# Attention scores in slots of three units instead of two, in a fused threshold-attention and SwiGLU kernel

## The chip, the cores and the metric

One core of a Trainium2 chip (trn2) runs the whole program. The metric is device time in microseconds (us). TensorE is called PE in the profile, and its weight loads PEld; VectorE is DVE, ScalarE is ACT, GpSimd is POOL, and SP issues the DMAs.

## The reference

Attention with a cut close to each row's maximum, and then a feed-forward block on its output, all in fp32 (8 batches, 8 heads, 576 tokens, head dimension 64; 4608 tokens by 512 go through 512 x 1536 weights and back):

```python
scores = (q @ k.T) / sqrt(64)
thresh = max(scores) - tau                 # per row, tau = 0.02
attn   = exp(scores - max) where scores >= thresh, else 0
attn   = attn / (sum(attn) + 1e-9)
x      = (attn @ v) laid out as (batch*token, head*dim)     # 4608 x 512
out    = (silu(x @ w_gate) * (x @ w_val)) @ w_out           # 512 x 1536, 1536 x 512
```

## The kernel before

Heads are taken in pairs: a batch has four pairs, and there are 32 pairs. The first four (batch 0) run in an older form at the head of the program; the other 28 are "halved" pairs (list `halved`), each of which is cut into slots. The change is about these slots.

**A unit** is 64 queries of both heads against all 576 keys. Its scores lie on 128 partitions: two groups of 32 queries times two halves of the keys, 288 keys in the free dimension. A row's two halves stand in different groups of 32 partitions, so its maximum and its sum have to be exchanged between neighbouring groups. A pair has nine units.

**A slot** is `slot_scores` plus `slot_rest`. Four slots of a pair take two units each and the fifth (`t == NT`) takes one, so a batch has 20 slots and the 28 pairs have 140. One unit's scores are eight matmuls of a 64x32 array tile over 288 columns (L1513), and fill two PSUM banks, one for each head. There are two such tiles of two banks (pool `ps_s`), so that a slot of two units fills both. Then, in order:

- DVE takes the maximum of each unit (L1535); four small instructions exchange it between partition groups, on DVE (L1541) or on ACT (L1547, slots in `MAX_BY_ACT` and `FIRST_MAX_BY_ACT`), and DVE combines them (L1542, L1551);
- ACT makes the threshold (L1554), and for each head of each unit ACT makes the exponentials (L1558) and DVE the masks with their sum (L1559); both read the scores in PSUM;
- ACT exchanges the sums (L1571, four copies), DVE makes the reciprocals (L1576, L1577), and ACT (L1587) or POOL (L1584) scales;
- DVE transposes the slot's result in one instruction (L1588).

When the masks of a unit are done its PSUM tile is free. `sc_users` holds these masks, and the next scores into this tile wait for them. When all slots of a pair are turned, `attend` multiplies by v on PE (L1608, 72 matmuls) and ACT copies the result into the token matrix x.

**What PE does between slots.** The feed-forward block of the batch before is cut into steps, and `block_part` hands them out by tables, slot by slot: `GV` (gates and values, `Group` with its seven products p1 to p7, all at L937), `CH` and `CD` (outputs: `Outputs` with po at L1103, and `Deep` with px at L1305 and py at L1317), and for the first halved batch `PLAIN` (`plain_group`, pg and pv at L1037) and `CH0`. A chunk of 512 tokens has six groups of gates and values for each of two halves of 256 tokens. In the head, `block` makes the first five groups of the first half of chunk 0 (L515) beside the attention of batch 0; `plain_group` makes the sixth and the second half later.

**What sets the order.** PE's instructions are issued in the order of the program. Those of DVE, ACT, POOL and SP are jobs of a planner (`Plan`), which knows a duration for each, and issues the one that can start first; a lower `rank` goes first. Planned durations decide the order alone. The jobs up to the masks have rank 0; exchanging the sums, scaling and transposing come later (rank 1 or 2). All engines run their instructions in the order issued, so a job that waits holds up what is behind it on its engine.

After the last slot two more pairs of banks are given to the feed-forward block (`more_banks`), and the last two chunks run without attention beside them.

Of the kernel before, what the change touches and what calls it, by code (L numbers as in the profile page):

```python
# [112 lines left out]
def kernel(  # L113
# [26 lines left out]
    SH = S // 2  # L140
    TC = 256
# [7 lines left out]
    assert 2 * D == P and NCC == NP == 4 and D == 2 * G and S - SM == 2 * G and SM == 2 * TC and B == 2 * BT and QA == TC  # L149
# [14 lines left out]
    sums = deque(const.tile([P, 4, 3], F32, name=f"sums{i}") for i in range(4))  # L164
# [11 lines left out]
    PB = 26  # L176
# [216 lines left out]
    def statistics(*names):  # L393
        return [stp.tile([P, 4, 2] if x == "mx" else [P, 4], F32, name=x) for x in names]
# [166 lines left out]
    FIRST = "full", 0  # L561
    ready = deque()

    def cost(unit):
        return 2 * (NF - GR) * HCOST
# [3 lines left out]
    def block():  # L569
        while True:  # L570
            if not ready:
                yield 0
                continue
            unit = ready.popleft()
            gts = {}
            for f in range(0, NF - GR, GR):
                yield from gate(unit, f, gts)
                yield from value(unit, f, gts)
# [20 lines left out]
    segs += [{"i": i, "tiles": ([2, 3, 0, 1] if i % 2 else [0, 1, 2, 3]) + [NT], "halved": True} for i in range(NP, NPAIR)]  # L599
# [320 lines left out]
    class Group:  # L920
# [64 lines left out]
        def finish(self, t, gb, gj, hold, mv):  # L985
            n, old = turn_of(n_bufs)
            ht = hall[:, t, self.g]
            rank = 0 if self.g == NF2 - 1 and t == 0 else 1
# [10 lines left out]
        def p3(self):  # L999
# [3 lines left out]
                                                                        op1=ALU.add), m, self.u1, rank=0 if self.g == NF2 - 1 else 1)  # L1003
# [229 lines left out]
    class Deep:  # L1233
# [151 lines left out]
        def gates_end(self):  # L1385
            state["last_product"]()
            self.late(plan.t + plan.PIPE)
# [104 lines left out]
    sc_users = deque([[], []])  # L1492
    sum_users = deque([[] for _ in range(4)])

    def slot_scores(seg, t):

        plan.force(*seg["qk"])
        qT, kT = seg["qT"], seg["kT"]
        q0 = t * P
        nu = 2 if t < NT else 1  # L1500
        pss, marks = [], []
        for u in range(nu):
            deps, sc_users[0] = sc_users[0], []
            sc_users.rotate(-1)

            def fn():
                ps = ps_s.tile([P, 2, 512], F32, name="sc")
                pss.append(ps)
                for g in range(NG):
                    a, c = divmod(g, 2)  # L1510
                    for h, hs in enumerate(heads):
                        col = q0 + u * D + a * G
                        nc.tensor.matmul(ps[g * G:(g + 1) * G, h, 0:SH], qT[hs, col:col + G],  # L1513
                                         kT[hs, c * SH:(c + 1) * SH], start=True, stop=True)

            marks.append(pe(0.7, fn, *deps, *seg["qk"]))
        return pss, marks

    turned_jobs = {}

    def slot_rest(seg, t, pss, marks, by_act, max_by_act):
        m = 2 * len(pss)
# [5 lines left out]
        scs = [ps[:, h, 0:SH] for ps in pss for h in range(2)]  # L1528
        base, order = seg["p"]
        first = order(t)  # L1530
        ps = [pall[:, base + (first + x) * SH:base + (first + x + 1) * SH] for x in range(m)]
        whole = pall[:, base + first * SH:base + (first + m) * SH]
        rs = []
        for x, tile_ in enumerate(pss):
            rs.append(job("DVE", 0.72, lambda x=x, tile_=tile_: nc.vector.tensor_reduce(  # L1535
                out=mx[:, 2 * x:2 * x + 2, 0], in_=tile_[:, :, 0:SH], axis=AX.X, op=ALU.max, negate=True), marks[x], rank=0))
# [17 lines left out]
        tj = job("ACT", 0.25, lambda: nc.scalar.activation(th[:, 0:m], nm[:, 0:m], AF.Identity, bias=cut, scale=-1.0), nj, rank=0)  # L1554
        masks, users = [], [[] for _ in pss]
        ej = tj
        for x in range(m):
            ej = job("ACT", 0.42, lambda x=x: nc.scalar.activation(ps[x], scs[x], AF.Exp, bias=nm[:, x:x + 1]), ej, rank=0)  # L1558
            mj = job("DVE", 0.45, lambda x=x: nc.vector.scalar_tensor_tensor(  # L1559
                out=ps[x], in0=scs[x], scalar=th[:, x:x + 1], in1=ps[x], op0=ALU.is_ge, op1=ALU.mult, accum_out=sm[:, x, 0:1]),  # L1560
                ej, *old_sums, rank=0)
            masks.append(mj)
            users[x // 2].append(mj)
        for u in users:
            sc_users[0] = u
            sc_users.rotate(-1)
# [6 lines left out]
        xj = job("ACT", 0.78, exchange, *masks, rank=1)  # L1573
# [7 lines left out]
        scaled = []  # L1581
        for x in range(m):
            if x % 2 and t < NT and not by_act:
                scaled.append(job("POOL", 1.02, lambda x=x: nc.gpsimd.tensor_scalar(  # L1584
                    out=ps[x], in0=ps[x], scalar1=ri[:, x:x + 1], scalar2=None, op0=ALU.mult), rj, rank=1))
            else:
                scaled.append(job("ACT", 0.46, lambda x=x: nc.scalar.activation(ps[x], ps[x], AF.Copy, scale=ri[:, x:x + 1]), rj, rank=2))  # L1587
        seg["turned"].append(job("DVE", 0.72 * len(pss), lambda: nc.vector.transpose(out=whole, in_=whole), *scaled, rank=2 if t < NT else 1))  # L1588
# [4 lines left out]
    def attend(seg):  # L1593
        i = seg["i"]
        b, cc = divmod(i, NP)
        base, _ = seg["p"]
# [3 lines left out]
        holds = [take("xa") for _ in range(R)]  # L1600

# [14 lines left out]
        lo = G if i % 2 else 0  # L1616
        at_last = 0 if i % 2 else 2 * NT * G
# [44 lines left out]
    for seg in halved:  # L1662
        seg["turned"] = []
        seg["p"] = (8 * SH, lambda t: 4 * t + 2 if t < NT else 0) if seg["i"] % 2 else (0, lambda t: 4 * t)
# [29 lines left out]

    def gv_steps(n):
# [8 lines left out]
    GV = {2: 3, 3: 4, 4: 2, 5: 5, 6: 1, 7: 3, 8: 3, 9: 2, 10: 5, 11: 2, 12: 3, 13: 3, 14: 5}  # L1704
    CH = {16: 3, 17: 2, 18: 2, 19: 1, 0: 2, 1: 2}
    BY_ACT = (0, 1, 4, 5, 9, 10, 12, 13, 14, 15, 16, 18)
    MAX_BY_ACT = (10,)
    FIRST_BY_ACT = (3, 6, 13, 14, 18, 19, 21, 22, 23, 25, 28, 29, 30, 31, 32, 38)
    FIRST_MAX_BY_ACT = (0, 7, 9, 10, 23, 30, 35, 36, 40, 41)
    CD = {15: 2, 16: 2, 17: 1, 18: 1, 19: 1, 0: 1}  # L1710
    PLAIN = {5: 2, 6: 0, 10: 1, 11: 0, 0: 1, 1: 1, 2: 1, 3: 1, 4: 2, 7: 1, 8: 1, 9: 1, 12: 1, 13: 1}
    CH0 = {14: 1, 15: 3, 17: 2, 18: 2, 19: 2, 20: 3, 21: 1}
# [8 lines left out]
    def block_part(b, kk):  # L1721
        s = (b - 1) * 20 + kk
        if s == 0:
            state["gv"] = chain(plain_group(0, NF2 - 1, u_bufs), *(plain_group(1, g, n_bufs) for g in range(NF2)))
        if s < 20 + LAG:
            gv_steps(PLAIN.get(s, 1) if s < 14 else 0)
# [3 lines left out]
            elif s == 13:  # L1730
# [3 lines left out]
        c = b - 1  # L1734
        if kk in GV:
            if kk == 2:
                state["gv"] = gates_and_values(c)
            gv_steps(GV[kk])
            if c == DEEP and kk < 2 + len(NESTED):
                deepen(NESTED[kk - 2], plan.t, *(j for js in plain_stores.values() for j in js), *summed)  # L1740
            if kk == 14:
                next(state["gv"], None)
                begin_outputs(c)
        elif kk == 15 and c < DEEP:
            out_steps(1)
            state["last_product"]()
# [112 lines left out]
```

## Time and profile before

| | |
|---|---|
| time, median of 3 runs | 1424.97 us (1423.84 to 1427.69) |
| the profiled execution: its time, its span | 1423.61 us, 1421.8 us |
| mean granted clock of PE in it | 0.994 |
| PE busy | 1383.3 us (97%) |
| DVE, ACT, POOL busy | 1072.7 us (75%), 874.9 us (62%), 716.5 us (50%) |
| head (batch 0) | 0 to 141 us |
| the seven halved batches | 141 to 1184 us |
| tail, no attention beside it | 1184 to 1422 us |

The page gives each engine's busy time, and groups of instructions by the line of the kernel, with count and mean duration. The timeline lists instructions in order of start; `x8` behind a row means eight merged ones, and a bracket gives the idle time ahead of them and what ended it. One fp32 matmul of the program appears as two rows' worth of instructions (2016 score matmuls are x4032). Matmuls overlap, so the time that a block of them takes from PE is the distance from its first start to the start of what follows it.

### The profile page before, as it was taken

To read this page: it belongs to the slowest core of one execution; us is meant where nothing else is said; L and a number is where in the kernel's file an instruction comes from. 1 tells how busy PE (TensorE), PEld (TensorE's weight loads), DVE (VectorE), ACT (ScalarE), POOL (GpSimd) and SP (SyncE) were. 2 spreads that over 40 slices of the span, in tenths; PEclk is the share of its full clock that TensorE was granted. 3 is DMA by queue.
4 is the path that set the end of the run, shared out by engine and by line. 5 is a ranking of instruction groups with operands and counts; after the bars stand their busy time and mean duration, and the time that the engine had idled before them with its cause. 6 is when DMAs were issued, how large, how long until landed. Compare 5 with 4: busy or idle time off the path is not lost.

```text
span 1421.8 us, 36646 instructions
## 1 busy us (share of the span) xinstructions
PE 1383.3 (97%) x14142; PEld 1089.8 (77%) x14142; DVE 1072.7 (75%) x3011; ACT 874.9 (62%) x2377; POOL 716.5 (50%) x666
## 2 busy tenths in 40 slices
PE   9999898999999999999999999999999999999997
PEld 6676666777777778777787788777877788899897
DVE  7988789888867887888878876987688864365364
ACT  6888667567756677677757765777576764221220
POOL 2465668844373859634874478445944493000000
PEclk9999899999999999999999999999999999999999
DMA  8734214455314541544154523553155403424411
GB/s 172 213 124 132 59 32 128 127 193 151 100 47 118 155 109 42 165 127 138 30 160 127 139 56 123 129 141 89 54 168 138 109 25 133 154 81 138 153 52 31
DMA packets 208382, 162.17 MB, mean 114 GB/s; under 512 B 166224, under 2 KB 180560, under 8 KB 202832
## 3 DMA queue, kind: packets, MB, share of 16 engines
q1 hardware_dynamic: 204608, 159.39, 39.5%
q8 instruction: 113, 1.85, 0.5%
q10 hardware_dynamic: 3600, 0.43, 0.2%
q14 instruction: 61, 0.50, 0.1%
HBM read 138.28 MB, written 21.50 MB: 112 GB/s over the span
## 4 chain that ended last, share of the span: by engine, by line
PE 77%; DVE 12%; ACT 5%; SPq 2%; issue 2%; DMA 1%; ACTq 0%; DVEq 0%
PE pb L937 16%; PE pe L937 11%; PE pa L937 10%; PE px L1305 10%; PE sc L1513 9%; PE xa L1608 7%; PE py L1317 4%; PE po L1103 4%; DVE pall L1559 3%; PE sc L937 2%; DVE mx L1535 2%; ACT pall L1558 2%; DVE pall L1588 1%; DVE mx L1541 1%; SPq L334 1%
## 5 line engine op out<-in xcount | busy, mean ns | idle before, releaser
L1559 DVE SCALAR_TENSOR_TENSOR pall<-sc,th,pall 128x288 f32<-128x288 f32 x504 | 233.2, 510 | 71.6 <-ACT pall L1558 70.8
L937 PE MATMUL pb<-xall,big 128*128 128x256 f32 x1032 | 247.6, 383 | 0.0
L1558 ACT ACTIVATE pall<-sc,nm 128x288 f32<-128x288 f32 x504 | 214.3, 495 | 16.7 <-DVE pall L1559 16.6
L937 PEld LDWEIGHTS pb<-xall,big 128*128 128x128 f32 x1032 | 192.6, 190 | 41.3 <-issue 8.4
L1535 DVE TENSOR_REDUCE mx<-sc 128x2 f32<-128x576 f32 x252 | 179.3, 744 | 39.0 <-PE sc L1513 38.0
L1587 ACT ACTIVATE pall<-pall,ri 128x288 f32<-128x288 f32 x396 | 186.5, 528 | 14.7 <-DVE ri L1577 12.9
L1588 DVE STREAM_TRANSPOSE pall<-pall 128x1152 f32<-128x1152 f32 (+1 forms) x140 | 174.9, 1251 | 15.0 <-ACT pall L1587 14.3
L1513 PE MATMUL sc<-kT,qT 64*32 64x288 f32 x4032 | 162.7, 413 | 18.5 <-DVE pall L1559 15.1
L937 PE MATMUL pa<-xall,big 128*128 128x256 f32 x752 | 180.1, 382 | 0.0
L937 PE MATMUL pe<-xall,big 128*128 128x256 f32 x752 | 179.5, 381 | 0.0
L937 PEld LDWEIGHTS pa<-xall,big 128*128 128x128 f32 x752 | 140.8, 190 | 29.3 <-ACT tmp L960 5.1
L937 PEld LDWEIGHTS pe<-xall,big 128*128 128x128 f32 x752 | 141.4, 190 | 26.9 <-issue 5.6
L1584 POOL TENSOR_SCALAR pall<-pall,ri 128x288 f32<-128x288 f32 x108 | 108.1, 1014 | 106.8 <-DVE ri L1577 106.8
L1554 ACT ACTIVATE th<-nm,cut 128x4 f32<-128x4 f32 (+1 forms) x140 | 41.3, 295 | 178.7 <-DVE nm L1542 166.1
L792 POOL TENSOR_TENSOR hall<-hall,tmp 128x512 f32<-128x512 f32 x79 | 100.6, 1277 | 92.5 <-DVE hall L990 45.4
L1571 ACT COPY sums<-sums 32x4 f32<-32x4 f32 (+1 forms) x560 | 108.5, 194 | 49.2 <-DVE pall L1559 41.3
L1608 PE MATMUL xa<-pall,vall 64*32 64x288 f32 x4032 | 131.3, 403 | 0.2 <-PE sc L1513 0.2
L1513 PEld LDWEIGHTS sc<-kT,qT 64*32 64x32 f32 x4032 | 57.8, 106 | 92.7 <-issue 49.4
L1608 PEld LDWEIGHTS xa<-pall,vall 64*32 64x32 f32 x4032 | 90.5, 107 | 35.4 <-DVE hall L990 1.7
L792 POOL TENSOR_TENSOR tmp<-tmp 128x512 f32<-128x512 f32 x36 | 46.0, 1279 | 76.7 <-ACT tmp L1012 76.7
L1541 DVE TENSOR_REDUCE mx<-mx 32x4 f32<-32x4 f32 (+1 forms) x508 | 75.5, 149 | 9.4
L989 ACT ACTIVATE vall<-tmp 128x512 f32<-128x512 f32 x96 | 60.4, 633 | 28.2 <-DVE tmp L1002 25.2
(223 smaller groups left out, 2379.4 us busy)
## 6 DMA issues: line engine op xcount, KB each, us to landing
big<-sums_hbm SPq DMA_DIRECT2D x42, 1024.0 KB, 5.2
big<-sums_hbm SPq DMA_DIRECT2D x48, 768.0 KB, 4.9
vall<-in_v_dram SPq DMA_DIRECT2D x112, 144.0 KB, 3.0
out_dram<-big SPq DMA_DIRECT2D x32, 256.0 KB, 2.5
qT<-in_q_dram SPq DMA_DIRECT2D x112, 72.0 KB, 4.7
kT<-in_k_dram SPq DMA_DIRECT2D x112, 72.0 KB, 2.9
wo<-in_moe_w_gate_dram SPq DMA_DIRECT2D x16, 384.0 KB, 3.9
wo<-in_moe_w_val_dram SPq DMA_DIRECT2D x16, 384.0 KB, 4.3
```

What stands on the lines that cost most here:

```text
L792: return lambda: nc.gpsimd.tensor_tensor(out=out, in0=a, in1=b, op=op)
L937: nc.tensor.matmul(ps[:, i], w[:, k_, i * P:(i + 1) * P], x[:, k_, :], start=first and i == k_ == 0, stop=True, skip_group_check=True)
L1305: nc.tensor.matmul(ps, a[:, f, :], ws[n][:, f, :], start=bank_ not in begun, stop=True, skip_group_check=True)
L1513: nc.tensor.matmul(ps[g * G:(g + 1) * G, h, 0:SH], qT[hs, col:col + G], kT[hs, c * SH:(c + 1) * SH], start=True, stop=True)
L1535: rs.append(job("DVE", 0.72, lambda x=x, tile_=tile_: nc.vector.tensor_reduce(out=mx[:, 2 * x:2 * x + 2, 0], in_=tile_[:, :, 0:SH], axis=A ...
L1558: ej = job("ACT", 0.42, lambda x=x: nc.scalar.activation(ps[x], scs[x], AF.Exp, bias=nm[:, x:x + 1]), ej, rank=0)
L1559: mj = job("DVE", 0.45, lambda x=x: nc.vector.scalar_tensor_tensor(out=ps[x], in0=scs[x], scalar=th[:, x:x + 1], in1=ps[x], op0=ALU.is_ge, ...
L1571: nc.scalar.copy(sm[g * G:(g + 1) * G, 0:m, 1], sm[o * G:(o + 1) * G, 0:m, 0])
L1584: scaled.append(job("POOL", 1.02, lambda x=x: nc.gpsimd.tensor_scalar(out=ps[x], in0=ps[x], scalar1=ri[:, x:x + 1], scalar2=None, op0=ALU. ...
L1587: scaled.append(job("ACT", 0.46, lambda x=x: nc.scalar.activation(ps[x], ps[x], AF.Copy, scale=ri[:, x:x + 1]), rj, rank=2))
L1588: seg["turned"].append(job("DVE", 0.72 * len(pss), lambda: nc.vector.transpose(out=whole, in_=whole), *scaled, rank=2 if t < NT else 1))
L1608: nc.tensor.matmul(holds[a].ap()[x * G:(x + 1) * G, 0:SH].rearrange("d (i q) -> d i q", q=G), vr[rs, h, j, ds], p[rs, h, :, j, :], start=( ...
```

## The change

A slot now takes three units, so that a pair has three slots, a batch 12 and the 28 pairs 84. The four banks stay: each head has a tile of two banks, the first two units lie in columns 0 to 287 of one bank each, and the third is cut into halves of 144 keys, which lie in columns 288 to 431 of both banks. The scores of the third unit are therefore 16 matmuls of 144 columns in place of 8 of 288. All scores of a slot are issued together and wait for all masks of the slot before.

The maxima of a slot are four instructions in place of two; the exchanges, thresholds, sums and reciprocals are made for six columns at a time in place of four (or two). The exponentials of the third unit come after the masks of the first two units of the same head. Transposes are made by unit. `attend` now comes ahead of the scores of the next pair's second slot, where it came behind them. The p buffer has 24 in place of 26 places.

All tables by slot are new, for 12 slots a batch. `block` in the head makes four groups in place of five; `plain_group` makes one more.

```diff
-    PB = 26
+    PB = 24
+    IN_HEAD = 4
...
-            for f in range(0, NF - GR, GR):
+            for f in range(0, GR * IN_HEAD, GR):
...
     def slot_scores(seg, t):
...
-        for u in range(nu):
-            deps, sc_users[0] = sc_users[0], []
-            sc_users.rotate(-1)
-            def fn():
-                ps = ps_s.tile([P, 2, 512], F32, name="sc")
...
-            marks.append(pe(0.7, fn, *deps, *seg["qk"]))
+        deps, sc_users[:] = sc_users[:], []
+        def fn():
+            pss.extend(ps_s.tile([P, 2, 512], F32, name="sc") for _ in heads)
+            for u, part, keys in ((0, (0, slice(0, SH)), (0, SH)), (1, (1, slice(0, SH)), (0, SH)),
+                                  (2, (0, slice(SH, SH + SQ)), (0, SQ)), (2, (1, slice(SH, SH + SQ)), (SQ, SH))):
                 for g in range(NG):
                     a, c = divmod(g, 2)
                     for h, hs in enumerate(heads):
+                        col = (NU3 * t + u) * D + a * G
+                        nc.tensor.matmul(pss[h][(slice(g * G, (g + 1) * G), *part)], qT[hs, col:col + G],
+                                         kT[hs, c * SH + keys[0]:c * SH + keys[1]], start=True, stop=True)
+        return pss, pe(1.85, fn, *deps, *seg["qk"])
...
+        for h, tile_ in enumerate(pss):
+            n = n_of(h, 0)
+            rs.append(job("DVE", 0.72, lambda n=n, tile_=tile_: nc.vector.tensor_reduce(
+                out=mx[:, n:n + 2, 0], in_=tile_[:, :, 0:SH], axis=AX.X, op=ALU.max, negate=True), mark, rank=0))
+            rs.append(job("DVE", 0.42, lambda n=n, tile_=tile_: nc.vector.tensor_reduce(
+                out=mx[:, n + 2:n + 3, 0], in_=tile_[:, :, SH:SH + SQ], axis=AX.XY, op=ALU.max, negate=True), mark, rank=0))
...
+            ej = job("ACT", 0.42, lambda x=x, n=n: nc.scalar.activation(ps[x], scs[x], AF.Exp, bias=nm[:, n:n + 1]), ej,
+                     *((masks[h, 0], masks[h, 1]) if u == 2 else ()), rank=0)
...
-        seg["turned"].append(job("DVE", 0.72 * len(pss), lambda: nc.vector.transpose(out=whole, in_=whole), *scaled, rank=2 if t < NT else 1))
+        for u in range(NU3):
...
+            seg["turned"].append(job("DVE", 0.72, lambda both=both: nc.vector.transpose(out=both, in_=both), *scaled, rank=rank))
...
-    GV = {2: 3, 3: 4, 4: 2, 5: 5, 6: 1, 7: 3, 8: 3, 9: 2, 10: 5, 11: 2, 12: 3, 13: 3, 14: 5}
-    CH = {16: 3, 17: 2, 18: 2, 19: 1, 0: 2, 1: 2}
-    CD = {15: 2, 16: 2, 17: 1, 18: 1, 19: 1, 0: 1}
+    GV = {1: 2, 2: 7, 3: 4, 4: 5, 5: 6, 6: 5, 7: 6, 8: 6, 9: 0}
+    CH = {0: 2, 1: 5, 9: 1, 10: 3, 11: 2}
+    CD = {0: 1, 1: 1, 9: 2, 10: 2, 11: 2}
+    POOLED = {1: 3, 3: 2, 6: 3, 7: 2, 11: 1}
+    MAX_BY_ACT = (0, 3, 5, 6, 8, 9, 10)
...
+    PLAIN = {0: 1, 1: 3, 2: 2, 3: 2, 4: 2, 5: 3, 6: 1, 7: 2}
+    CH0 = {8: 3, 9: 2, 10: 4, 11: 3, 12: 2}
...
+        if x == 1 and n > 0:
+            prepare_v(seg, attend(halved[n - 1]))
+        pss, mark = slot_scores(seg, t)
```

## The prediction

> **What bounds the kernel now.** I read the page first (shares by engine), then PE's timeline for the price of a block of scores, then the busy times in stretches and PE's waits for where it still stands idle, and last DVE's and ACT's timeline through one slot.
>
> The page, section 1, and two groups of section 5:
>
> ```profile
> PE 1383.3 (97%) x14142; PEld 1089.8 (77%) x14142; DVE 1072.7 (75%) x3011; ACT 874.9 (62%) x2377; POOL 716.5 (50%) x666
> ...
> L1535 DVE TENSOR_REDUCE mx<-sc 128x2 f32<-128x576 f32 x252 | 179.3, 744 | 39.0 <-PE sc L1513 38.0
> ...
> L1513 PE MATMUL sc<-kT,qT 64*32 64x288 f32 x4032 | 162.7, 413 | 18.5 <-DVE pall L1559 15.1
> ```
>
> PE is the bound: 38.5 us of idle time in all, half of it just ahead of scores. DVE and ACT have room on average. So a gain must come from PE's own time, and a loss from PE waiting.
>
> Busy time by stretches (us, columns PE, PEld, DVE, ACT, POOL, granted PE clock, DMA): first, second, third and fourth halved batch.
>
> ```profile
> 141.00:278.00 137.00, 124.37 (x1417) 87.99 (x1424) 117.68 (x354) 88.14 (x270) 105.04 (x97) 0.95 0.30 82
> 278.00:431.00 153.00, 151.71 (x1664) 113.48 (x1656) 120.41 (x359) 102.81 (x301) 75.42 (x78) 1.00 0.45 124
> 431.00:587.00 156.00, 154.70 (x1749) 120.68 (x1745) 123.39 (x377) 103.28 (x296) 106.68 (x102) 1.00 0.41 116
> 587.00:738.00 151.00, 149.98 (x1760) 116.66 (x1766) 121.08 (x372) 104.71 (x301) 89.89 (x85) 1.00 0.42 115
> ```
>
> From the second batch on PE stands idle about 1 us a batch. Only the first batch (12.6 us idle, clock 0.95, so another 6.9 us) and the head have slack.
>
> PE's timeline around two slots:
>
> ```profile
> 615.27 0.71 PE L1513 MATMUL sc<-kT,qT 64*32 64x288 f32 x16
> 615.91 1.99 PE L937 MATMUL pb<-xall,big 128*128 128x256 f32 x8
> 617.75 1.89 PE L937 MATMUL pe<-xall,big 128*128 128x256 f32 x8
> 619.57 1.20 PE L1513 MATMUL sc<-kT,qT 64*32 64x288 f32 x32
> 620.70 1.99 PE L937 MATMUL pa<-xall,big 128*128 128x256 f32 x8
> 622.53 1.89 PE L937 MATMUL pb<-xall,big 128*128 128x256 f32 x8
> 624.25 1.89 PE L937 MATMUL pe<-xall,big 128*128 128x256 f32 x8
> ```
>
> Start to start, one unit takes 0.64 us and two take 1.13: 0.49 for the unit added, 0.15 fixed. Beside it, the product behind scores takes 1.83 instead of 1.73, and the product ahead of scores 1.82: a boundary of 0.19. So a block of scores costs 0.34 us besides its units.
>
> **The change, part by part.** Times are against the profiled execution (1423.6 us, span 1421.8); the median shown is 1.4 above it, which I add at the end.
>
> *Score blocks.* Before, 28 blocks of one unit and 112 of two: 28 x 0.64 + 112 x 1.13 = 144.5 us, and 140 boundaries x 0.19 = 26.6. After, 84 blocks of three: 1.13 + third unit + 0.19. The third unit has the same columns but 16 matmuls of 144 in place of 8 of 288. This is not in the trace. It can't be under 0.49, as the columns are the same. A rule speaks against it: the Trainium skill, "TensorE: Matmul & The Clock Gate", section "Wait — 56ns, not 53.3ns?", says that matmuls never start closer than about 25 ns, however short. The 16 matmuls are 32 rows of the trace, so by the rule an estimated 32 x 25 = 0.80 us, and 84 x 0.31 = 26 us more than the columns need. The trace cut to the first 0.14 us of a block:
>
> ```profile
> 619.57 0.47 PE L1513 MATMUL sc<-kT,qT 64*32 64x288 f32 x8
> ```
>
> Eight matmuls start and end within 0.47 us, and one lasts 0.40 to 0.43 (median 403 ns): the eight array tiles start within 47 ns, 7 ns apart. Where tiles run side by side the 25 ns don't hold. Eight tiles of 144 columns need 120 ns a round (half of the 243 between rounds of 288 in this block), more than 47. I take 0.51. After: 84 x (1.64 + 0.19) = 153.7. Difference: 153.7 - 171.1 = **-17.4 us**. This is PE time in a stretch where PE is 99% busy, so it is all on the path.
>
> *Waiting for the banks.* Before, each of two tiles came free by itself; now a slot's scores wait for all six masks of the slot before. So I compare the chain from scores to last mask with the work that PE has in between. The chain of a two-unit slot, from the scores that end at 630.6:
>
> ```profile
> 630.35 1.42 DVE L1535 TENSOR_REDUCE mx<-sc 128x2 f32<-128x576 f32 x2 [0.29 <-PE sc L1513]
> 631.81 0.63 DVE L1541 TENSOR_REDUCE mx<-mx 32x4 f32<-32x4 f32 x4
> 632.48 0.16 DVE L1542 TENSOR_REDUCE nm<-mx 128x4 f32<-128x8 f32 x1
> ...
> 632.67 0.30 ACT L1554 ACTIVATE th<-nm,cut 128x4 f32<-128x4 f32 x1 [2.47 <-DVE nm L1542]
> 632.88 1.66 ACT L1558 ACTIVATE pall<-sc,nm 128x288 f32<-128x288 f32 x4
> ```
>
> The last mask ends at 635.6: 4.9 us; in the steady batches the slots have 5.6 as median and 7.2 at most. For three units: reductions 2 x 0.74 + 2 x 0.42 (half the elements of 0.74, plus a little) = 2.3, starting only when all scores are done (+0.4); exchange and combination 0.9; threshold and first exponential 0.7; six masks at 0.57 (0.44 apart here when nothing waits, and the third unit's exponentials wait for masks) 3.4. That is 7.5, and with one or two transposes or gate instructions of DVE in between (0.7 each, partly in gaps) 8 to 8.6.
>
> PE's work between slots, counted from the new order with 0.4325 us a matmul of 256 columns, 0.224 of 128 and 4.5 for an `attend`: in a steady batch, from its slot 0 on, 9.2, 8.2, 12.1, 11.4, 8.7, 10.4, 13.2, 10.4, 10.4, 10.9, 9.9, 9.9 us. All but slot 1 cover 8.6. In slot 1, DVE's masks lie interleaved with four additions that wait for the px product (4.7 us after the scores), so I take 8.7 and 0.5 us of stall for each of five batches: 2.5. In the first halved batches the cover is thinner: slots 0, 2, 4, 7, 8 have 5.8, 6.9, 6.9, 6.9, 7.8; slot 1 of the second batch 3.5, its last two 7.8 and 5.2. Against 8.6 (9.9 for slot 0, where weight joins lie ahead of the masks on DVE) and 0.1 of boundary that is 4.0 + 1.6 + 1.6 + 1.6 + 0.7 + 5.0 + 0.7 + 3.3 = 18.5. Together 21 us.
>
> Before: all blocks of scores took 156.8 us start to start, 12.3 over the 144.5, and the idle time ahead of them was 12.0; about 3 of these 24 are the slow clock, so 21 are stalls. **Net 0**: the old stalls of the first batch go, and new ones come in the same place.
>
> *The clock.* In the first batch PE ran below full clock after idle times of 1.7, 3.6 and 1.0 us: 6.9 us lost. The Trainium skill (same page, "What's actually happening") has the clock fall only after an idle window of about 3.4 us; by that, only the stalls of 4.0 and 5.0 us count, an estimated 1.7 us each. The trace shows slow products after shorter idle times too: after 0.96 and 0.51 us of idle time a pg block took
>
> ```profile
> 198.45 5.41 PE L1037 MATMUL pg<-xall,big 128*128 128x256 f32 x16
> ```
>
> where 3.72 is usual. I follow the trace: about as much lost as before, **0** (by the rule -3.5).
>
> *The moved group.* 16 matmuls x 0.4325 = 6.9 us of PE work leave the head and come in the first halved batch, where they count in full. (The words of the change say the second batch; counted from zero it is batch 1.) The head from 61 to 141 us has PE busy 93%, DVE 85%, ACT 82%; per slot 6.7 us would become 6.1, close to the 6.2 to 6.5 of the earlier slots that have no fill. I take 4.4 of 6.9 back: **+2.5** (bounds 0 and +6.9).
>
> *Late attends.* In the early batches a pair's last slot is followed by `attend` after 14.8 us of PE work; mask chain 8.6, exchange and sums 1.3, five or six scalings at 0.53, transposes 3 x 0.77 come to 15, with the next slot's reductions in between. **+2** (0 to 6). In steady batches there are 16.4 us or more.
>
> *Other engines.* DVE: exchanges 508 to 144 x 0.15 us, transposes 140 instructions (175.0 us) to 252 x 0.77, net about 50 us less. ACT about 20 less, POOL 88 scalings for 108. SP has the same 614 issues; q and k of the next pair are asked for at its first slot, some 40 us ahead (landing 4.7 us), v right after `attend`, now ahead of scores. POOL's weight sums and stores are pushed into slots 2 to 15 from 4 to 28 and rank last; the first batch's POOL (77% busy) loses seven scalings. All this is worth 0 as long as DVE and ACT keep up; if not, it shows as a longer chain, priced below.
>
> Sum: -17.4 + 0 + 0 + 2.5 + 2 = -13. On the profile's time 1410.7, on the median's 1412.
>
> **The rivals.**
>
> *Slower: the four banks as one.* Once all six masks free the banks together, the chain decides in every slot that has less cover than it. If DVE or ACT run in bursts and the chain is 10.1 instead of 8.6: nine early slots lose 1.5 more (13.5), and five steady batches lose 3.8 more each in slots 0, 1, 4 and a little in three others (19): +32, **1444**. The gain is gone from a chain of about 9.3 on. For: the slot of 141 us needed 8.3 already with four tiles, and DVE was 86% busy in the first batch. Against: in steady batches four-tile chains are within 7.2.
>
> *Short matmuls at 25 ns apart.* +24 us, **1436**. Against: the eight starts in 47 ns.
>
> *The start of the program eats it.* The head gives nothing back (+4.4) and the longer stalls double the time at half clock (+7): **1423**. For: the clock was lost in just this stretch.
>
> *It does not do what it says* can be excluded: the order on PE has 84 blocks of scores.
>
> **How the numbers follow.** Main forecast 0.62 (its own range 1404 to 1420), banks as one 0.17, start 0.14, short matmuls 0.04, better than forecast (early stalls absent, 1398) 0.03. A measurement of this kernel can tell about 0.3% (4.3 us) from no change. Faster: 0.62 + 0.03 + a quarter of the start case, 0.69. Same: half of the start case and short chains, 0.12. Slower: the rest, 0.19. The range is 1399 to 1430: it leaves out most of the two slow rivals and little below.
>
> **What would show it.** Right: scores x5376 rows with a block at about 1.64 us start to start; steady batches of about 148 us for 150.4; PE's waits for the masks mostly before 300 us. Wrong: waits for the masks in steady batches over 2 us each; third units over 0.6 us; a head that still ends at 141 us; a clock under 0.95 in the first batch.

## The result, and the profile after

| | before | after |
|---|---|---|
| time, median | 1424.53 us (1423.84 to 1427.69, 4 runs) | 1404.17 us (1403.55 to 1406.35, 4 runs) |
| ratio, 95% interval | | 0.9856 [0.9837, 0.9874] |
| profiled execution: its time, its span | 1423.61, 1421.8 us | 1406.35, 1404.5 us |
| PE busy, idle | 1383.3, 38.5 us | 1365.8, 38.7 us |
| mean granted clock of PE | 0.994 | 0.994 |

The change makes the kernel 1.4% faster: 20.4 us between the medians, 17.3 us between the two profiled spans (the profiled execution of after is the slowest of its four). The lines of the page that answer to those shown of before, section 1 and two groups of section 5 (busy us and mean ns behind the bar, then the idle time just before and what ended most of it):

```profile
PE 1365.8 (97%) x15486; PEld 1118.0 (80%) x15486; DVE 1023.4 (73%) x2680; ACT 867.4 (62%) x2257; POOL 693.3 (49%) x641
...
L1514 PE MATMUL sc<-kT,qT 64*32 64x144 f32 (+1 forms) x5376 | 153.6, 350 | 15.2 <-DVE pall L1562 10.3
...
L1535 DVE TENSOR_REDUCE mx<-sc 128x2 f32<-128x576 f32 x168 | 124.4, 740 | 35.4 <-PE sc L1514 35.0
```

PE is busy 17.5 us less, and its idle time and its clock are the same in total. So the whole difference of the spans lies in PE's own work. In the total of the idle time two changes cancel: ahead of scores it fell from 18.5 to 15.2 us, and in the head it rose from 9.5 to 13.4. DVE's busy time fell by 49 us and POOL's by 23; whether that was worth anything is tested below.

Busy time by stretches of after (us; PE, PEld, DVE, ACT, POOL, granted PE clock, DMA share, GB/s): the first five halved batches.

```profile
140.90:273.70 132.80, 128.24 (x1655) 100.67 (x1656) 113.07 (x325) 89.03 (x245) 102.86 (x94) 0.99 0.36 97
273.70:422.10 148.40, 138.52 (x1790) 109.50 (x1790) 112.56 (x314) 97.80 (x272) 69.74 (x71) 0.98 0.41 115
422.10:580.40 158.30, 156.88 (x1938) 127.41 (x1938) 115.44 (x326) 103.96 (x287) 107.45 (x105) 1.00 0.39 106
580.40:727.30 146.90, 146.74 (x1944) 119.93 (x1944) 113.30 (x319) 103.80 (x285) 86.94 (x83) 1.00 0.43 117
727.30:874.10 146.80, 146.64 (x1939) 119.91 (x1938) 113.29 (x319) 103.71 (x285) 86.80 (x83) 1.00 0.43 117
```

Read it against the rows of before. The two steady batches shown (from 580 us) take 146.9 and 146.8 us for 150.4, and PE stands idle 0.2 us in each for 1.0. The first halved batch takes 132.8 us for 136.6 although it does a group more; its idle time fell from 12.6 to 4.6 us and its clock rose from 0.95 to 0.99. The second batch now has what the first has lost: 9.9 us of idle time for 1.3, at a clock of 0.98. The third batch is 1.6 us longer and the last slots are shorter, which fits new tables that deal out the output steps differently among the batches (not tested): from the last batch's start to the end of the program it is 381.8 us for 382.9. The head ends at 140.9 us for 141.1.

PE's timeline through two slots of a steady batch:

```profile
613.42 1.89 PE L940 MATMUL pe<-xall,big 128*128 128x256 f32 x8
615.24 1.72 PE L1514 MATMUL sc<-kT,qT 64*32 64x288 f32 x64
616.89 1.99 PE L940 MATMUL pa<-xall,big 128*128 128x256 f32 x8
618.72 1.89 PE L940 MATMUL pb<-xall,big 128*128 128x256 f32 x8
```

A block of three units takes 1.65 us from start to start (the median of all is 1.65 too). The product behind it takes 1.83 and the product ahead of it 1.82 where 1.73 is usual: the boundary is as before. The chain of the slot before, on DVE, whose scores end at 602.96:

```profile
605.28 0.64 DVE L1543 TENSOR_REDUCE mx<-mx 32x6 f32<-32x6 f32 x4
605.96 0.17 DVE L1544 TENSOR_REDUCE nm<-mx 128x6 f32<-128x12 f32 x1
606.04 0.77 DVE L1590 STREAM_TRANSPOSE pall<-pall 128x576 f32<-128x576 f32 x1
606.88 0.52 DVE L1562 SCALAR_TENSOR_TENSOR pall<-sc,th,pall 128x288 f32<-128x288 f32 x1
...
611.25 0.52 DVE L1562 SCALAR_TENSOR_TENSOR pall<-sc,th,pall 128x288 f32<-128x288 f32 x1 [0.21 <-ACT pall L1560]
```

The last mask ends at 611.8, 8.8 us after the scores. This time from the end of a slot's scores to the end of its last mask is called the chain below; its median in the steady slots is 8.4 us, and the longest is 9.9. PE's next scores come at 615.24, so the banks have been free for 3.5 us.

PE's waits in after (us in total, times, longest), and the second batch where the one long wait is, by the timelines of PE, DVE and SP:

```profile
PE sc L1514 <- DVE pall L1562: 10.3, 3, 7.5
PE pv L517 <- ACT big L477: 6.5, 4, 2.3
PE sc L1514 <- issue: 4.7, 4, 1.7
```

```profile
285.08 1.70 PE L1514 MATMUL sc<-kT,qT 64*32 64x288 f32 x64
...
298.41 3.58 PE L1514 MATMUL sc<-kT,qT 64*32 64x288 f32 x64 [7.48 <-DVE pall L1562]
```

```profile
289.22 0.78 DVE L1652 STREAM_TRANSPOSE kT<-kT 128x576 f32<-128x576 f32 x1 [4.83 <-DMA kT<-in_k_dram]
...
291.24 0.72 DVE L1535 TENSOR_REDUCE mx<-sc 128x2 f32<-128x576 f32 x1
```

```profile
265.78 3.42 SPq L862 DMA_DIRECT2D sums_hbm<-big  x4
269.30 4.83 SPq L867 DMA_DIRECT2D big<-sums_hbm  x2
274.18 3.66 SPq L862 DMA_DIRECT2D sums_hbm<-big  x4
277.89 4.80 SPq L336 DMA_DIRECT2D qT<-in_q_dram  x4
282.73 3.00 SPq L336 DMA_DIRECT2D kT<-in_k_dram  x4
```

Read from the bottom up: SP issues eight stores of weight sums and a load of them in two DMAs ahead of q and k of the next pair, and is done with k's DMAs at 285.7 us. DVE has k's transpose next in its order, and stands for 4.8 us until k lands. The maxima of the slot are behind that transpose: the scores end at 286.7, and their first maximum starts at 291.24. Then the slot's masks are late, and the next slot's scores wait 7.5 us. They then take 3.58 us for 1.7: PE's clock has fallen to about half (granted clock 0.55 from 298.4 to 302.0 us).

### The profile page after: what moved, and what is told of

It is laid out like the page before. It is cut to its first block, busy times and chain, and to the rows that moved or that the text cites. A ratio compares the mean times of both kernels' runs of the same rounds, so it can differ in the third digit from the quotient of the medians.

```text
span 1404.5 us, 38812 instructions
## 1 busy us (share of the span) xinstructions
PE 1365.8 (97%) x15486; PEld 1118.0 (80%) x15486; DVE 1023.4 (73%) x2680; ACT 867.4 (62%) x2257; POOL 693.3 (49%) x641
## 4 chain that ended last, share of the span: by engine, by line
PE 77%; DVE 1%; SPq 1%; issue 1%; DMA 0%; POOL 0%; ACT 0%; DVEq 0%; ACTq 0%
PE pb L940 17%; PE pa L940 12%; PE pe L940 12%; PE px L1308 11%; PE sc L1514 8%; PE xa L1611 8%; PE py L1320 5%; PE po L1106 3%; PE sc L940 1%; SPq L336 1%; DVE big L798 0%; PE sc L1308 0%; SPq L1370 0%; DVE hall L993 0%; DMA sums_hbm<-big 0%
## 5 line engine op out<-in xcount | busy, mean ns | idle before, releaser
L1560 ACT ACTIVATE pall<-sc,nm 128x288 f32<-128x288 f32 x504 | 231.7, 497 | 34.3 <-DVE pall L1562 33.9
L1590 DVE STREAM_TRANSPOSE pall<-pall 128x576 f32<-128x576 f32 x252 | 189.1, 763 | 62.6 <-ACT pall L1588 44.2
L1514 PE MATMUL sc<-kT,qT 64*32 64x144 f32 (+1 forms) x5376 | 153.6, 350 | 15.2 <-DVE pall L1562 10.3
L1514 PEld LDWEIGHTS sc<-kT,qT 64*32 64x32 f32 x5376 | 100.9, 107 | 69.4 <-issue 31.3
L1535 DVE TENSOR_REDUCE mx<-sc 128x2 f32<-128x576 f32 x168 | 124.4, 740 | 35.4 <-PE sc L1514 35.0
L1585 POOL TENSOR_SCALAR pall<-pall,ri 128x288 f32<-128x288 f32 x88 | 88.1, 1013 | 68.7 <-DVE ri L1576 56.9
L1570 ACT COPY sums<-sums 32x6 f32<-32x6 f32 x336 | 66.6, 198 | 45.5 <-DVE pall L1562 40.9
L1320 PE MATMUL py<-wo,hall 128*128 128x256 f32 x336 | 74.8, 379 | 0.0
L1549 ACT COPY mx<-mx 32x6 f32<-32x6 f32 x192 | 37.3, 194 | 60.5 <-DVE mx L1537 58.6
L1537 DVE TENSOR_REDUCE mx<-sc 128x1 f32<-128x288 f32 x168 | 74.4, 443 | 0.0
```

Of the source, the lines that this page charges most:

```text
L1320: nc.tensor.matmul(ps, a[:, f, i * P:(i + 1) * P], operands[o][:, f, :], start=first and i == f == 0, stop=True, skip_group_check=True)
L1514: nc.tensor.matmul(pss[h][(slice(g * G, (g + 1) * G), *part)], qT[hs, col:col + G], kT[hs, c * SH + keys[0]:c * SH + keys[1]], start=True, ...
L1535: rs.append(job("DVE", 0.72, lambda n=n, tile_=tile_: nc.vector.tensor_reduce(out=mx[:, n:n + 2, 0], in_=tile_[:, :, 0:SH], axis=AX.X, op= ...
L1560: ej = job("ACT", 0.42, lambda x=x, n=n: nc.scalar.activation(ps[x], scs[x], AF.Exp, bias=nm[:, n:n + 1]), ej, *((masks[h, 0], masks[h, 1] ...
L1585: scaled.append(job("POOL", 1.02, lambda x=x, n=n: nc.gpsimd.tensor_scalar(out=x, in0=x, scalar1=ri[:, n:n + 1], scalar2=None, op0=ALU.mul ...
L1590: seg["turned"].append(job("DVE", 0.72, lambda both=both: nc.vector.transpose(out=both, in_=both), *scaled, rank=rank))
```

## The experiments

Each time is against runs of the kernel before on the same chip (1424.99 to 1425.47 us as median). "After" without a number is the 1404.2 us of the result; run again beside the last two experiments, the changed kernel took 1403.5.

**The price of a block.** Six slots in each of the last six halved batches, 36 in all, have their scores cut in two blocks with a product in between; all else stays.

```diff
+        if between:
+            pe(1.3, lambda: fn(1), *deps, *seg["qk"])
+            between()
+            return pss, pe(0.7, lambda: fn(2))
...
+    SPLIT = 2, 3, 5, 6, 7, 8
...
-            gv_steps(GV[kk])
+            gv_steps(GV[kk] - (kk in SPLIT))
...
-        pss, mark = slot_scores(seg, t)
+        pss, mark = slot_scores(seg, t, (lambda: gv_steps(1)) if b > 1 and kk in SPLIT else None)
```

Here `fn(1)` makes the scores of the first two units, and `fn(2)` those of the third.

> The changed kernel, with the scores of six of the twelve slots in batches 2 to 7 (36 slots) cut in two blocks: two units, then one product of the gates (1.73 us), then the third unit. Nothing else is added: PE does the same matmuls. Theory (the gain is the 0.34 us that each block of scores costs besides its units, 0.15 at its start and 0.19 at its boundary): 36 blocks more cost 36 x 0.34 = 12 us, so about 1416 where the changed kernel has 1404; the slots are chosen so that the work between them still covers the chain to the masks, and PE's waits for masks stay as they are. Rival (the gain comes from fewer small instructions on DVE and ACT and fewer slots, not from fewer blocks): no small instruction is added, so the time stays within 2 us of 1404.

Measured: 1417.49 us (1415.62 to 1420.04), ratio 0.995 [0.9931, 0.9969]: 13.3 us above after, 0.37 a block (0.34 if each kernel is taken against its own runs of before). PE's timeline:

```profile
612.72 1.89 PE L940 MATMUL pe<-xall,big 128*128 128x256 f32 x8
614.54 1.20 PE L1516 MATMUL sc<-kT,qT 64*32 64x288 f32 x32
615.67 1.99 PE L940 MATMUL pa<-xall,big 128*128 128x256 f32 x8
617.60 0.72 PE L1516 MATMUL sc<-kT,qT 64*32 64x144 f32 x32
618.25 1.99 PE L940 MATMUL pb<-xall,big 128*128 128x256 f32 x8
620.08 1.89 PE L940 MATMUL pe<-xall,big 128*128 128x256 f32 x8
```

Two blocks take 1.13 and 0.65 where one took 1.65. The product between them takes 1.93, where the one behind an uncut block takes 1.83, and the product behind the second takes 1.83 where 1.73 is usual: 0.13 + 0.10 + 0.10 = 0.33 us more, for 0.34 predicted. PE's waits for masks did not grow (7.5 us in 3 waits), and its busy time rose by 14.0 us, from 1365.8 to 1379.8. So the number of blocks alone moves the time by about what the prediction charged. A steady batch grew by 3.0 us for six cuts, one more than these sums; some blocks there take 1.40 or 1.57 us for 1.13, and why was not followed.

**Shorter matmuls.** The third unit's scores in quarters of 72 keys in place of halves of 144: 32 matmuls for 16, the same columns.

```diff
-                                  (2, (0, slice(SH, SH + SQ)), (0, SQ)), (2, (1, slice(SH, SH + SQ)), (SQ, SH))):
+                                  *((2, (x // 2, slice(SH + x % 2 * (SQ // 2), SH + (x % 2 + 1) * (SQ // 2))),
+                                     (x * (SQ // 2), (x + 1) * (SQ // 2))) for x in range(4))):
```

> The changed kernel, with the third unit's scores in quarters of 72 keys instead of halves of 144: 32 matmuls instead of 16, the same columns. Theory (short matmuls on eight array tiles side by side start 7 ns apart, so they are bound by columns until a round of eight takes less than about 50 ns; 72 columns are 60 ns): the block stays at 1.65 to 1.75 us, the kernel within 0 to 8 us of 1404. Rival (the trace's 7 ns hide a floor of about 25 ns a matmul, or weight loads of 105 ns bound each round): the third unit goes from 0.5 to 0.85 us (weight loads, 8 rounds of 105 ns) or 1.6 us (25 ns each), 84 times, so 1433 or 1496.

Measured: 1423.61 us (1419.96 to 1426.53), ratio 0.9986 [0.997, 1.0002]. The whole gain is gone. Page and timeline:

```profile
L1515 PE MATMUL sc<-kT,qT 64*32 64x72 f32 (+1 forms) x8064 | 171.0, 292 | 15.0 <-DVE pall L1563 9.7
```

```profile
624.71 1.92 PE L1515 MATMUL sc<-kT,qT 64*32 64x288 f32 x96
626.57 1.99 PE L940 MATMUL pa<-xall,big 128*128 128x256 f32 x8
```

A block takes 1.86 us for 1.65, which is 17.6 us over 84 blocks, of 19.4 measured. The third unit is then 8 rounds in 0.73 us, 90 ns a round; by its columns a round of 72 is a quarter of the 243 ns between rounds of 288, 60 ns. So the expectation, that columns still decide at a quarter, was missed: the 19.4 us lie between its 0 to 8 and the 29 of the rival that blames weight loads. At halves they do decide: 0.52 us for the third unit (1.65 less 1.13), and 0.49 by columns. What sets the 90 ns is open. The floor of about 25 ns between any two starts, which the Trainium skill states ("TensorE: Matmul & The Clock Gate", section "Wait — 56ns, not 53.3ns?"), would make an estimated 1.6 us of these 64, so it isn't that.

**Small instructions on the chain.** All exchanges of maxima and sums are made twice.

```diff
-            for g in range(NG):
+            for g in [*range(NG)] * 2:
...
```

The same edit stands in all three exchanges; the planner's durations stay as they were.

> The changed kernel, with each exchange between partition groups (of maxima and of sums; four small instructions per slot each, 0.15 us on DVE, 0.2 on ACT) done twice, as many small instructions a batch as 24 slots would have. Theory (PE sets the time; small instructions count only where they push the chain to the last mask over the work between slots): the chain grows by 0.7 us, which is over the slack in the nine early slots and in slots 0 and 1 of steady batches, so 4 to 8 us, 1408 to 1412, in waits for masks. Rival (the small instructions saved are the gain): all of the gain is lost, 1420 to 1425.

Measured: 1474.16 us (1473.47 to 1475.63), ratio 1.035 [1.033, 1.0369]. It costs 70 us, and both expectations were far off. A steady batch takes 157.0 us, 10.2 more, and the chain's median is 10.0 us. PE's waits:

```profile
PE sc L1514 <- DVE pall L1562: 15.9, 10, 5.3
PE pb L940 <- ACT tmp L1015: 11.9, 12, 1.6
PE pb L940 <- ACT tmp L984: 8.3, 7, 1.4
```

Two of the three largest waits are of the feed-forward products, for their own results to be taken away by ACT. That was a cost that neither theory had. PE's busy time rose as well, from 1365.8 to 1386.3 us.

**A longer chain alone.** The maxima are combined ten times: nine more DVE instructions of 0.165 us in each slot, all on the chain.

```diff
-            nc.vector.tensor_reduce(out=nm[:, 0:m], in_=mx[:, 0:m, :], axis=AX.X, op=ALU.min)
+            combine()
+
+        def combine():
+            for _ in range(10):
+                nc.vector.tensor_reduce(out=nm[:, 0:m], in_=mx[:, 0:m, :], axis=AX.X, op=ALU.min)
...
```

> The changed kernel, with the maxima combined ten times instead of once in each slot (nine more DVE instructions of 0.16 us in the chain to the masks, 1.5 us). Prediction's rival of the four banks as one, with its price: a chain of 10.1 us for 8.6 costs 32 us, of which 19 in the five steady batches, so about 1436. From the slacks between last mask and next scores in the trace of the changed kernel I work out 15 us in the first 36 slots and 13 in the 48 after, 28 in all: 1432. Rival (a longer chain is hidden, as four-unit-wide slots leave PE 8 to 16 us of work): under 8 us, 1412.

Measured: 1500.05 us (1499.47 to 1503.87), ratio 1.0534 [1.0513, 1.0555]. The chain's median is 10.4 us, nearly the 10.1 of the prediction's rival, but the price is 96 us in place of 32. (What the expectation calls four-unit-wide slots are the slots of three units.) A steady batch takes 160.3 us, 13.4 more or 1.1 a slot. PE's waits in the whole kernel:

```profile
PE sc L1514 <- DVE pall L1566: 27.8, 19, 5.6
PE pb L940 <- ACT tmp L984: 16.4, 18, 1.4
PE sc L1514 <- issue: 15.2, 10, 3.5
```

The comparison of chain and cover (PE's work between two slots' scores) finds only the first line. The second is feed-forward work: its evacuations on ACT (the copies of PE's results out of PSUM) come behind the slot's threshold and exponentials in ACT's order, and when these come later, so do they, also in slots where PE's cover is ample. ACT and PE in a slot with 13 us of cover:

```profile
651.92 0.30 ACT L1560 ACTIVATE th<-nm,cut 128x6 f32<-128x6 f32 x1 [3.38 <-DVE nm L1548]
652.13 0.48 ACT L1564 ACTIVATE pall<-sc,nm 128x288 f32<-128x288 f32 x1
652.51 0.59 ACT L984 ACTIVATE tmp<-pb 128x512 f32<-128x512 f32 x1
```

```profile
649.02 1.89 PE L940 MATMUL pb<-xall,big 128*128 128x256 f32 x8
650.74 1.89 PE L940 MATMUL pe<-xall,big 128*128 128x256 f32 x8
653.15 1.99 PE L940 MATMUL pb<-xall,big 128*128 128x256 f32 x8 [0.52 <-ACT tmp L984]
```

ACT stands for 3.38 us until the maxima are combined; only behind the threshold and the first exponential does it take away a product that PE had finished at about 650.9, and the next product into these banks waits for it.

Waits are not all of the price. Of the 93.2 us between the two profiled spans, PE's idle time takes 62.9 (101.6 for 38.7) and its busy time 30.3 (1396.1 for 1365.8), with the same matmuls. About 5 of the 30.3 are clock, by the granted clock while PE is busy. Another part is that a block of scores behind a wait is itself longer:

```profile
684.98 2.13 PE L1514 MATMUL sc<-kT,qT 64*32 64x288 f32 x64 [0.47 <-DVE pall L1566]
687.04 1.99 PE L940 MATMUL pe<-xall,big 128*128 128x256 f32 x8
```

From start to start this is 2.06 us for 1.65. All 23 blocks here that waited over 0.15 us and ran at full clock took 2.06 us or more; why was not followed.

Is it the order, or the chain? The kernel with the longer chain, with the planner told of the true durations, so that it orders DVE and ACT for it (the lines taken out are those of the changed kernel):

```diff
-            nj = job("DVE", 0.18, lambda: nc.vector.tensor_reduce(out=nm[:, 0:m], in_=mx[:, 0:m, :], axis=AX.X, op=ALU.min), oj, rank=0)
+            nj = job("DVE", 1.73, combine, oj, rank=0)
...
-            nj = job("DVE", 0.82, largest, *rs, rank=0)
+            nj = job("DVE", 2.37, largest, *rs, rank=0)
```

> The kernel with the maxima combined ten times, whose time came out at 1500, with the planner told of it (2.37 and 1.73 us in place of 0.82 and 0.18), so that DVE's and ACT's jobs are put in another order; PE's order is the same. Theory (the 96 us come from work of the feed-forward block that stands behind the late masks and exponentials in the fixed order): the order gives most of it back, 1425 to 1455. Rival (the chain itself is too long for the four banks, as the prediction's rival has it): 1485 to 1500.

Measured: 1473.43 us (1472.15 to 1474.83), ratio 1.0337 [1.0319, 1.0354]. Between the two expectations: a better order gives back 27 of the 96 us, and 69 stay. The chain's median is still 10.4 us, but the waits of pb for ACT (21.1 us in the lines of L984 and L1015) are down to 0.9. How the 69 us divide between the chain and DVE's added load (0.165 x 9 x 84 = 125 us of busy time) is not separated.

**A shorter chain.** The exchanges of maxima and sums between partition groups are left out, so this kernel leaves out a part of the softmax.

```diff
-            for g in range(NG):
-                o = g ^ 1
-                nc.vector.tensor_reduce(out=mx[g * G:(g + 1) * G, 0:m, 1], in_=mx[o * G:(o + 1) * G, 0:m, 0:1], axis=AX.X, op=ALU.max)
-            nc.vector.tensor_reduce(out=nm[:, 0:m], in_=mx[:, 0:m, :], axis=AX.X, op=ALU.min)
+            nc.vector.tensor_reduce(out=nm[:, 0:m], in_=mx[:, 0:m, 0:1], axis=AX.X, op=ALU.min)
...
-        xj = job("ACT", 0.78, exchange, *masks.values(), rank=1)
...
-        rj = job("DVE", 0.36, total, xj, rank=1)
+        rj = job("DVE", 0.36, total, *masks.values(), rank=1)
```

> The changed kernel without the exchanges of maxima and sums between partition groups (each half of the keys has its own maximum and sum, which leaves out part of the softmax): 144 x 0.15 us less on DVE, 192 + 336 x 0.2 us less on ACT, the chain to the masks 0.7 us shorter. Theory (PE's own time is the bound now): only the early stalls shrink, 2 to 6 us, 1398 to 1402; steady batches stay at 146 to 147. Rival (DVE's and ACT's small instructions still cost time): 10 us or more, under 1394.

Measured: 1402.14 us (1401.83 to 1402.58), ratio 0.9837 [0.9823, 0.9852]. Page, section 1, and a stretch of steady batch:

```profile
PE 1365.0 (97%) x15486; PEld 1118.7 (80%) x15486; DVE 1014.4 (72%) x2536; ACT 764.8 (55%) x1729; POOL 692.1 (49%) x641
```

```profile
580.00:727.00 147.00, 146.84 (x1942) 120.04 (x1941) 112.63 (x300) 88.85 (x208) 86.75 (x82) 1.00 0.43 117
```

ACT is busy 103 us less, the chain's median is 7.4 us for 8.4, and the time falls by 2 us, which the intervals do not tell from no change. In the steady batch PE is 100% busy with and without. So the small instructions of DVE and ACT that the change saved are not where its gain comes from, and a chain that fits is worth nothing more when shortened.

**The moved group.** Five groups in the head, as before, and one group less in the first halved batch.

```diff
-    IN_HEAD = 4
+    IN_HEAD = 5
...
-    PLAIN = {0: 1, 1: 3, 2: 2, 3: 2, 4: 2, 5: 3, 6: 1, 7: 2}
+    PLAIN = {0: 1, 1: 3, 2: 2, 3: 1, 4: 2, 5: 2, 6: 1, 7: 2}
```

> The changed kernel with the moved group back in the head (five groups there, as before; one step less in slots 3 and 5 of the first halved batch). The prediction's step (taking 6.9 us of PE work out of the head shortens it by 4.4): the head gets 4.4 us longer, the first halved batch 6.9 shorter, so 2 to 3 us faster, about 1402. The traces of before and after (head 141.1 and 140.9 us, though 6.9 us of PE work are gone) say instead that the head is not bound by PE: then it stays at 141 and the kernel gets 5 to 7 us faster, less a stall of up to 1 us in slot 5: 1398 to 1400. If the group's removal from the head was what fed the first batch, its stalls grow and the time does not fall: 1404 to 1408.

Measured: 1404.23 us (1402.81 to 1406.16), ratio 0.9853 [0.9838, 0.9868]: no difference from after. The head is 1.9 us longer and the first batch 1.5 us shorter. (In the other profiles here, whose heads make four groups, the head ends between 139.4 and 142.5 us, so 1.9 is hardly more than that spread.) In either place there is idle time that swallows most of a group.

**The long wait in the second batch.** The stores on SP's queue are issued four slots later.

```diff
-            store_plain(g, parts[g])
+        if 14 <= s < 14 + NF2:
+            store_plain(s - 14, parts[s - 14])
```

> The changed kernel with the stores of the plain weights (four DMA issues a group, 0.9 us each on SP's queue) in slots 14 to 19 instead of 10 to 15, behind the loads of q and k that slot 12 asks for. In the trace of the changed kernel DVE stands 4.8 us before the transpose of k in slot 13, with the slot's maxima behind it, and PE's longest wait (7.5 us) follows. Theory (that wait is made by SP's queue): the wait shrinks to about 3.5 (the slot's own chain of 7.5 against 3.5 us of work), and the clock loss behind it too: 4 to 6 us faster, 1398 to 1400. Rival (the thin work of slot 13 alone makes it): no change within 1.5 us.

Measured: 1401.75 us (1400.08 to 1402.62), ratio 0.9833 [0.9818, 0.9848]. The wait of that slot on PE's timeline:

```profile
294.24 3.62 PE L1514 MATMUL sc<-kT,qT 64*32 64x288 f32 x64 [3.62 <-DVE pall L1562]
```

It is 3.6 us for 7.5: DVE transposes k without waiting. The second batch takes 144.3 us for 148.4. So SP's queue was the cause of half of the wait in the profile shown; the rest is the thin cover (3.6 us of products) that the prediction had seen. In the second profile of the changed kernel (the next experiment's), DVE stands only 2.0 us for k and the wait is 5.2 us, so there the queue made a third of it. The time is 2.4 us under after, where 4 to 6 were expected, and by time alone the two are not told apart.

**The thin cover as well.** The edit above, and two steps of gates and values moved one slot earlier in the second batch.

```diff
+    SOONER = {1: 2, 2: -2}
...
-            gv_steps(GV[kk])
+            gv_steps(GV[kk] + (SOONER.get(kk, 0) if c == 1 else 0))
```

This, the edit above and the changed kernel itself ran side by side on one chip:

> The changed kernel once more, as the measure for the two beside it on the same chip: 1402 to 1406.

> The changed kernel with the stores in slots 14 to 19, on the same chip as the two others: 1400 to 1402.5, 2 to 4 us under the changed kernel.

> The changed kernel with the stores in slots 14 to 19, and in the second halved batch two product steps moved from slot 2 to slot 1, so that slot 1 has 6.9 us of work for PE instead of 3.5, and slot 2 8.7 instead of 12.1. Theory (the wait left in slot 1, 3.6 us, is the slot's chain of 7.5 against 3.5 of work, and the slow clock follows it): the wait falls under 1 us and the half clock of 3.4 us behind it goes: 4 to 5 us faster than with the stores alone, 1396 to 1398. Rival (something else stands behind this wait, or slot 2 now stalls as much): within 1.5 us of 1401.7.

Measured: the changed kernel 1403.51 us, ratio 0.9835 [0.982, 0.9851]; stores later 1400.54 us, 0.9824 [0.9809, 0.9839]; both edits **1394.68 us** (1394.53 to 1395.34), 0.9779 [0.9765, 0.9792], 5.9 us under the stores alone and clear of both others. PE's timeline of both edits at the place:

```profile
291.34 1.89 PE L940 MATMUL pb<-xall,big 128*128 128x256 f32 x8
293.40 0.64 PE L1514 MATMUL sc<-kT,qT 64*32 64x288 f32 x2 [0.17 <-DVE pall L1562]
294.54 1.69 PE L1514 MATMUL sc<-kT,qT 64*32 64x288 f32 x62 [0.49 <-DVE pall L1562]
296.16 1.99 PE L940 MATMUL pe<-xall,big 128*128 128x256 f32 x8
```

The wait is 0.7 us and the block runs at full clock: between 292 and 302 us the granted clock is 1.00, where it was 0.66 in after and 0.83 with the stores moved alone. The second batch takes 139.3 us, for 145.8 in the changed kernel's profile on the same chip and 148.4 in the one shown above. These 6.5 us are most of the 8.4 between the two spans on this chip; 1.1 more lie in the head and 1.7 in the sixth halved batch, whose cause was not followed. This is the fastest version, 2.2% below the kernel before.

## Why the prediction was right

The prediction was 1412 us with a range of 1399 to 1430; 1404.17 was measured, on the side that it gave and at the lower edge of its main forecast (1404 to 1420). The mechanism, fewer blocks of scores on a PE that is nearly always busy, is the one that the runs show. Two terms of its sum were wrong (the moved group and the late attends), and that the waits for the banks came out near nothing is in part luck. Step by step:

- **Score blocks, -17.4: right.** PE's busy time fell by 17.5 us, of which about 1 is clock. The block of three takes 1.65 us (1.64 predicted), and the block cut in two confirms a price of 0.33 to 0.37 for 0.34. A steady batch's PE busy time fell by 2.7 us, 17.4 / 7 is 2.5. The other parts of the change (the place of `attend`, the tables, the p buffer) were not run apart, but this sum leaves them little.
- **The third unit in halves, 0.51: right.** It took 0.52. The floor of about 25 ns in the Trainium skill ("TensorE: Matmul & The Clock Gate", section "Wait — 56ns, not 53.3ns?"), by which 32 rows would need an estimated 0.80 us, did not hold for eight array tiles side by side. But the trace's argument ("120 ns a round, more than the 47 ns of starts") may not be carried further: at 60 ns a round by columns, still over 47, the round took 90.
- **Waiting for the banks, net 0: near in the sum (-3.3), with two wrong terms in it that worked against each other, which is luck.** PE's idle time ahead of scores is 15.2 us for 18.5. The steady slots lose nothing (2.5 were charged; the chain of slot 1 has 7.6 us as median, not 8.7). Most early slots wait less than their 0.7 to 4.0. But the slot charged with 5.0 waited 7.5, and the reason is the step that put SP's queue at 0: "q and k of the next pair are asked for at its first slot, some 40 us ahead" was said of the request, while the issue stood behind eight stores and a load. The number of DMAs was the same, their order was not.
- **The clock, 0: right within about 1 us.** From the stretches' clocks, (1 - 0.95) x 137 is 6.9 us lost before. After, there are 3.4 us at half clock in the head (0.98 of 10 us and 0.85 of 10), 3.4 in the first batch (0.83 of 10) and 6.8 at the long wait (0.66 of 10). Half of the last stretch lies in the wait itself (clock 0.51 from 294.8 to 298.4 us, where PE has nothing to run), so three times 1.7 us are lost, 5.1; by the same count it was 6.2 before. The slow stretches of the head and the first batch come after waits of at most 2.5 us. So the -3.5 that the prediction estimated from the idle window of about 3.4 us in the Trainium skill ("TensorE: Matmul & The Clock Gate", section "What's actually happening") would have been wrong here too.
- **The moved group, +2.5: wrong, 0.** The step that failed is its place: I looked for its time in the head, where 4.4 of 6.9 should come back, and 0.2 came; PE there now waits for ACT (6.5 us at L517 for 3.4 at the same place before), and its idle time in the head rose by 3.9 us. A head that still ends at 141 us was one of the prediction's own signs of being wrong, and so much of its rival "the start of the program eats it" came true. And I charged it in full in the first batch, where the vanished stalls left it room: that batch got 3.8 us shorter with it. Five groups in the head give the same time.
- **Late attends, +2: wrong, 0.** All waits of `attend` together are 1.8 us, the longest 0.5.
- The two last are 4.5 us, about the whole distance between -13 and the -17.3 of the spans; the -3.3 ahead of scores and the 3.9 of the head cancel. The medians differ by 3 us more than the spans, which is the spread of single executions.
- **The rival "four banks as one"** was rightly held unlikely: the chain is 8.4 us. Its price was wrong by a factor of three. (Its list has eight early slots and not nine, but that is 1.5 of its 32 us.) The step that failed compared the chain with PE's cover, slot by slot; a chain of 10.4 us costs 96 us in the order planned for the shorter one and 69 in a new order. The feed-forward block's evacuations on ACT are delayed with it, and PE's blocks behind waits take longer.

## What to carry to other kernels

Where PE is nearly 100% busy in the steady stretch, count the blocks, not only the columns: each change to another array tiling and back cost 0.33 to 0.37 us here, and merging 140 blocks into 84 took 17.5 us off PE's busy time while its idle time stayed the same. Before merging, compare the chain of the other engines with PE's cover slot by slot; when the chain outgrows the order, expect more than the sum of these differences, as what is queued behind it on ACT and DVE comes late too. After merging, look at the first long wait and follow it to its end: here it led from PE through a transpose on DVE to the order of DMAs on SP, and two small moves in the order were worth 8.8 us.

## What was not expected of the hardware

- Rounds of eight 64x32 tiles: 243 ns at 288 columns, about 130 at 144, 90 at 72. Quarters fall off the proportion and cost 0.2 us a block.
- Half clock came in stretches of 3.4 us, or twice that, behind waits of about 2.5 us (3.4 us long), 3.6 us (3.4 us long) and 7.5 us (6.8 us long); after the 0.7 us at the same place of the fastest version there was none. But the length of the wait does not settle it: behind the head's wait of 2.3 us the clock fell in after (0.85 from 70 to 80 us) and not in before (1.00). What else decides is open.
- A block of 64x32 scores behind a wait takes 2.06 us from start to start for 1.65, at full clock: so the three such blocks of after and all 23 of the longer chain.
- Four DMA issues of q, of k or of sums take SP 3.0 to 4.8 us in a row in the profile shown, and the ten DMAs ahead of q and k took 11.9 us (3.42 + 4.83 + 3.66), which no engine's busy time shows. The time varies: the four of q took 2.9 us for 4.8 in the second profile of the same kernel.
